# A small fill on GpSimd between two indirect transfers in a row, in a linear-attention and top-1 expert kernel

## The chip, the cores and the metric

The kernel runs on one core of a Trainium2 chip. The metric is the device time of one execution in microseconds, as the median of three runs. The engines are TensorE (PE in the profile), VectorE (DVE), ScalarE (ACT), GpSimd (POOL), and SyncE (SP), which here only starts transfers.

## What is computed

```python
# attention without a softmax, 8 batches x 8 heads, 576 rows of 64
kv  = np.einsum('bhsd,bhse->bhde', k, v)
out = np.einsum('bhsd,bhde->bhse', q, kv)
rms = np.sqrt(np.mean(out * out, axis=-1, keepdims=True) + 1e-06)
x   = (out / rms * g_norm)      # -> 4608 tokens of 512
# top-1 mixture of 8 experts, inner width 1024
logits = x @ w_gate
expert_idx = argmax(logits);  gate_w = softmax(logits) at that expert
for e in range(8):
    xe = x[expert_idx == e]
    out[expert_idx == e] = gate_w * (relu(xe @ w1[e]) @ w2[e])
```

So each token goes to one expert, and the tokens have to be sorted by expert on the way. The kernel does the sorting with indirect transfers, which GpSimd starts.

## The kernel before

**Attention stage.** The 4608 tokens are worked in 36 steps `s` of 128 tokens, nine for each pair of batches `P`. A step transposes queries, multiplies them with the batch's `kv` matrix (L339), squares and normalises (L359 to L378), and leaves a row of 512 half-precision numbers, token number and gate weight in a tile `xg`. Every three to five steps a `Route` object works out for its steps which expert each token takes and which rank it has there; `send` writes the row numbers to `sli`. Then `scatter(t)` (L450) sends one step's 128 rows to their places in `xs_scratch` in HBM, one indirect transfer for each of the 36 steps.

All engines are ordered by hand: each list of small functions (`mid`, `late`, `last`) is emitted step by step, and each engine works its own instructions in that order. Two other things are on GpSimd in this stage: `heads` (L256), four copies for each batch that reorder queries, and `pace` (L492), a one-column copy that waits until VectorE has reached the same step. For the first three pairs of batches every scatter has a `pace` ahead of it; for the last pair there is none.

**The seam.** The last two scatters belong to the route `tail` and follow the last step. The first gather may only start once every scatter has landed, since it reads `xs_scratch`. Meanwhile ScalarE and VectorE turn the weights of experts 0 and 1 to half precision, and TensorE runs 24 products on zeros (`zeros`, L127).

**Expert stage.** Eight jobs, one for each expert, and a ninth for what is left over. A job has up to five tiles of 128 tokens (640 rows). `rows(n)` starts the five gathers of job `n` (`gather`, L630) into five of 16 buffers `xe`; `rows(0)` and `rows(1)` are started at the seam, and job `n` starts `rows(n + 2)`. `flip` (L658, L661) transposes a gathered tile; `one` (L677, L684) is the first matrix product with the ReLU, 16 groups of four products for a job; `two` (L691, L696) is the second product, scales by the gate weight into `ys` (8 buffers) and scatters the rows to the output (L699). The five tiles of job `n + 1` are flipped inside the second half of job `n`'s first product, one after each group from the third on:

```python
for f in range(8):
    job.one(ws, f)
    ...
    if ws == job.halves - 1 and f >= 2 and flips:
        nxt.flip(flips.pop(0))
```

The weights come through SyncE, 2 MB each for `w1` and `w2` of an expert. Those of job 2 wait for the third flip of job 0 (`hold=True`). Job `n` starts those of job `n + 2`, and VectorE turns `w1` of job `n + 1` to half precision (L168). So GpSimd's list in the expert stage is: ten gathers, five output scatters of job 0, five gathers, five scatters of job 1, and so on, all indirect transfers and nothing else.

Of the kernel before, what the change touches and what calls it, by code (L numbers as in the profile page):

```python
# [12 lines left out]
F16 = mybir.dt.float16  # L13
# [15 lines left out]
def kernel(  # L29
# [11 lines left out]
    nc = tc.nc  # L41
# [49 lines left out]
    P_const = ctx.enter_context(tc.tile_pool(name="pconst", bufs=1))  # L91
# [28 lines left out]
    ]  # L120
    tabi = P_const.tile([128, 2, 32], I32, tag="tabi")
    zero16 = P_const.tile([128, 128], F16, tag="zero16")

    def zeros(t, n):

        for _ in range(n):
            nc.tensor.matmul(t, zero16, _bc(zero16, 1, 4), start=True, stop=True)  # L127
# [60 lines left out]
    with (  # L188
# [62 lines left out]
        def heads(b, j):  # L251

            if j == 0:
                qp[b] = PA.tile([128, 4, 8, 64], F32, tag="qp", bufs=2, name="qp")
            tv = ld["q", b].rearrange("p h (j d) -> p h j d", j=4)
            nc.gpsimd.tensor_copy(qp[b][:, j, :, :], tv[:, :, j, :])  # L256


# [126 lines left out]
        class Route:  # L385
# [61 lines left out]
                csum.append(cs)  # L447

            def scatter(self, t):
                nc.gpsimd.indirect_dma_start(  # L450
                    out=xs_views[9 * self.P + self.g0 + t],
                    out_offset=IndirectOffsetOnAxis(ap=self.sli[:, t:t + 1], axis=0),
                    in_=xgs[self.P][:, self.g0 + t, :].bitcast(I32),
                    in_offset=None,
                )
# [12 lines left out]
        for b in range(1, B):  # L468
            f = first_slot[b]
            n = 4 if b % 2 else 5  # L470
            plan = [[0, 1], [2, 3]] if n == 4 else [[0], [1, 2], [3]]
            o = 1 if b < 3 else 0
            for m, ii in enumerate(plan):
                for i in ii:
                    at(late, f - n + m + o, kv_mm, b, i)
            at(late, f - 3 + o, kv_copy, b)
            if o:
                at(mid, f - 1, kv_t, b)
                at(late, f - 1, kv_gate, b)
            else:  # L480
                at(late, f - 2, kv_t, b)
                at(mid, f - 1, kv_gate, b)
            for j in range(4):
                at(last, f - 4 + j // 2, heads, b, j)
            if b + 2 < B:
                at(last, f - 2, load_batch, b + 2)
# [33 lines left out]
        for j in range(4):  # L520
            heads(0, j)
# [39 lines left out]
        tail.ranks()  # L561
        tail.send()
        for t in range(2):
            tail.scatter(t)
        cp = PSA.tile([128, 8], F32, tag="misc", bufs=1, name="cp")
        nc.tensor.matmul(cp, ones, csum[-1], start=True, stop=True)
# [16 lines left out]
    with (  # L583
# [43 lines left out]
            nc.vector.tensor_copy(tabi[:, 1, 0:8], oi)  # L627

        def gather(xe, rows):
            nc.gpsimd.indirect_dma_start(  # L630
                out=xe.bitcast(I32),
                out_offset=None,
                in_=xs.ap(),
                in_offset=IndirectOffsetOnAxis(ap=rows, axis=0),
                bounds_check=E * N - 1,
                oob_is_err=False,
            )

        class Job:
# [48 lines left out]
            def two(self, t):  # L688
                yp = PSF.tile([128, D], F32, tag="yp", bufs=3, name="yp")
                for f in range(8):  # L690
                    nc.tensor.matmul(  # L691
                        yp, self.ht[:, f, t * 128:(t + 1) * 128], self.w.w2[:, f, :],
                        start=(f == 0), stop=(f == 7),
                    )
                ys = PF.tile([128, D], F32, tag="ys", bufs=8, name="ys")
                nc.vector.tensor_scalar(  # L696
                    ys, yp, self.xe[t][:, 514:516].bitcast(F32), None, op0=ALU.mult
                )
                nc.gpsimd.indirect_dma_start(  # L699
                    out=self.views[t],  # L700
                    out_offset=IndirectOffsetOnAxis(ap=self.idx[:, t:t + 1], axis=0),
                    in_=ys,
                    in_offset=None,
                    bounds_check=N - 1,
                    oob_is_err=False,
                )

        def left_over(t, t0, view):

            ev = nc.values_load(  # L710
                tabi[0:1, 0, bass.ds(t, 1)], engines=[ENG.SP],
                min_val=0, max_val=E - 1,
            )
            okm = PF.tile([128, 1], F32, tag="okm", bufs=2, name="okm")
            nc.vector.tensor_tensor(okm, pcol, nvf[:, bass.ds(t, 1)], op=ALU.is_lt)
            bgm = PF.tile([128, 1], F32, tag="bgm", bufs=2, name="bgm")
            nc.vector.tensor_scalar(bgm, okm, -BIG, BIG, op0=ALU.mult, op1=ALU.add)
            gi = PF.tile([128, 1], I32, tag="gi", bufs=2, name="gi")
            nc.vector.scalar_tensor_tensor(
                out=gi, in0=tabb[:, bass.ds(t, 1)], scalar=pcol, in1=bgm,  # L720
                op0=ALU.add, op1=ALU.add,
            )
            gather(xe_bufs[t0], gi)
            return Job([xe_bufs[t0]], Weights(bass.ds(ev, 1)), okm, bgm, [view])

        with tc.manual_schedule(engines=by_hand):
            jobs = []
            for n, e in enumerate(order):
                if e == "left":
                    jobs.append(None)  # L730
                    continue
                jobs.append(Job(
                    [xe_bufs[(n % 3) * CT + t] for t in range(CT)], W[n],
                    valid[:, e, :], bigm[:, e, :], out_views[e * CT:(e + 1) * CT],
                ))

            def rows(n):
                if n < len(order) and order[n] != "left":
                    for t in range(CT):
                        gather(jobs[n].xe[t], rowi[:, order[n], t:t + 1])  # L740

            rows(0)
            rows(1)
            zp = PSF.tile([128, 512], F32, tag="yp", bufs=3, name="yp")
            zeros(zp, 24)
            for t in range(3):
                jobs[0].flip(t)
                zeros(zp, 2)

            W[2].stage1(hold=True)  # L750
            W[2].stage2(hold=True)

            for n in range(len(order)):
                job = jobs[n]
                if n == 4:
                    jobs[E] = left_over(0, 3 * CT, out_views[E * CT])
                    W[E] = jobs[E].w
                nxt = jobs[n + 1] if n + 1 < len(order) else None
                rows(n + 2)
                flips = list(range(nxt.nt)) if nxt is not None else []  # L760
                for ws in range(job.halves):
                    for f in range(8):
                        job.one(ws, f)
                        if n == 0 and ws == 0 and f in (3, 6):
                            job.flip(3 + f // 6)
                        if ws == job.halves - 1 and f >= 2 and flips:
                            nxt.flip(flips.pop(0))
                        if n > 0 and ws == 0 and f % 2 == 1 and nxt is not None:
                            W[n + 1].half1(nc.vector, f // 2)
                            if f == 7 and n + 2 < len(order):  # L770
                                W[n + 2].stage1()
                for kk in range(max(job.nt, 4)):
                    if kk < job.nt:
                        job.two(kk)
                    if n > 0 and kk < 4 and nxt is not None:
                        W[n + 1].half2(kk)
                        if kk == 3 and n + 2 < len(order):
                            W[n + 2].stage2()
                    if n == 0 and kk == 1:
                        left_over_table()  # L780
# [42 lines left out]
```

## Time and profile before

| | |
|---|---|
| median of three runs | 306.58 us (305.64 to 307.6) |
| span of the profiled run | 303.6 us |
| mean granted TensorE clock | 0.975 |
| indirect transfers to `xs_scratch` (L450) | 36, mean 983 ns on GpSimd |
| gathers to `xe` (L630) | 40, mean 1012 ns, and one for the left-over job |
| indirect transfers to the output (L699) | 41, mean 1038 ns |
| fill of a 128x576 tile on GpSimd (L517) | 4, mean 573 ns |

The time of an indirect transfer on GpSimd is the time in which the engine is busy with it. The data arrive later; the profile gives that as "DMA to landing", counted from the start on the engine. A line of a timeline has the start and the duration in microseconds, the engine, the line of the kernel, the operation, its result and its operands, and in brackets how long the engine had been idle before it and what ended that. "<-issue" means that it waited for nothing that the profile shows. A line of the table by stretches has the stretch, its length, then for each engine the busy time and the number of instructions, the granted clock of TensorE (1.00 is full), and the busy share and rate of the DMA engines.

### The profile page before, as it was taken

To read this page: it belongs to the slowest core of one execution; us is meant where nothing else is said; L and a number is where in the kernel's file an instruction comes from. 1 tells how busy PE (TensorE), PEld (TensorE's weight loads), DVE (VectorE), ACT (ScalarE), POOL (GpSimd) and SP (SyncE) were. 2 spreads that over 40 slices of the span, in tenths; PEclk is the share of its full clock that TensorE was granted. 3 is DMA by queue.
4 is the path that set the end of the run, shared out by engine and by line. 5 is a ranking of instruction groups with operands and counts; after the bars stand their busy time and mean duration, and the time that the engine had idled before them with its cause. 6 is when DMAs were issued, how large, how long until landed. Compare 5 with 4: busy or idle time off the path is not lost.

```text
span 303.6 us, 6229 instructions
## 1 busy us (share of the span) xinstructions
PE 275.5 (91%) x2349; PEld 189.7 (62%) x2349; DVE 164.0 (54%) x431; ACT 159.2 (52%) x342; POOL 153.2 (50%) x205
## 2 busy tenths in 40 slices
PE   8697989899989987647979999999999999999993
PEld 3376877788878886513644756647566574665652
DVE  0024576768778777781237946445464553556140
ACT  1024556556564665488530674737657365672831
POOL 9332016438636764665762576457365663215052
PEclk9799999999999999869999999999999999999998
DMA  6999999999999999922894299979799898968421
GB/s 188 341 284 279 243 279 349 301 276 351 333 299 315 386 401 405 367 105 71 268 364 171 86 367 305 399 220 393 282 346 347 266 388 276 353 279 270 167 101 66
DMA packets 59790, 85.66 MB, mean 282 GB/s; under 512 B 16493, under 2 KB 41326, under 8 KB 59760
## 3 DMA queue, kind: packets, MB, share of 16 engines
q1 hardware_dynamic: 50512, 65.10, 67.7%
q0 software_dynamic: 6976, 18.96, 17.2%
q10 hardware_dynamic: 2272, 1.20, 1.5%
q8 instruction: 19, 0.31, 0.4%
q14 instruction: 11, 0.09, 0.1%
HBM read 71.71 MB, written 15.50 MB: 287 GB/s over the span
## 4 chain that ended last, share of the span: by engine, by line
PE 30%; issue 10%; DMA 9%; POOL 4%; POOLq 1%
PE yp L691 14%; PE hp L677 14%; DMA out_dram<-ys,idx 7%; POOL out_dram L699 2%; DMA xe<-xs_scratch,rowi 2%; PE xp L658 2%; POOL xe L630 2%; POOLq L818 0%; POOL xs_scratch L450 0%; POOLq L699 0%; POOLq L630 0%; POOLq L783 0%
## 5 line engine op out<-in xcount | busy, mean ns | idle before, releaser
L684 ACT ACTIVATE ht<-hp 128x320 f16<-128x320 f32 (+1 forms) x136 | 57.9, 428 | 70.0 <-PE hp L677 58.6
L677 PE MATMUL hp<-xt,w1e 128*128 128x320 f16 (+1 forms) x544 | 79.3, 294 | 0.1
L699 POOL DMA_INDIRECT out_dram<-ys,idx x41 | 42.6, 1038 | 65.7 <-DVE ys L696 56.6
L691 PE MATMUL yp<-w2e,ht 128*128 128x512 f16 x328 | 72.3, 379 | 0.0
L677 PEld LDWEIGHTS <-w1e 128*128 128x128 f16 x544 | 50.3, 98 | 18.8 <-issue 0.6
L696 DVE TENSOR_SCALAR ys<-yp,xe 128x512 f32<-128x512 f32 x41 | 30.6, 750 | 47.2 <-PE yp L691 47.2
L691 PEld LDWEIGHTS <-ht 128*128 128x128 f16 x328 | 32.1, 98 | 37.2
L339 PE MATMUL op<-kvs,qts 128*128 128x144 f32 (+1 forms) x320 | 45.5, 301 | 5.5 <-ACT kvt L292 2.5
L630 POOL DMA_INDIRECT xe<-xs_scratch,rowi x40 | 40.5, 1012 | 14.4 <-issue 10.2
L339 PEld LDWEIGHTS op<-kvs,qts 128*128 128x128 f32 (+1 forms) x320 | 38.1, 184 | 9.0 <-ACT kvt L292 3.1
L450 POOL DMA_INDIRECT xs_scratch<-xg,sli x36 | 35.4, 983 | 13.3 <-issue 10.8
L661 DVE COPY xt<-xp 128x512 f16<-128x512 f16 x41 | 17.4, 425 | 37.2 <-PE xp L658 37.2
L256 POOL COPY qp<-ld 128x512 f32<-128x512 f32 x32 | 18.5, 614 | 32.1 <-DMA ld<-in_q_dram 30.0
L179 ACT CAST w2e<-ws 128x1024 f16<-128x1024 f32 x32 | 31.0, 1042 | 0.0
L359 ACT ACTIVATE sq<-op 128x512 f32<-128x512 f32 x36 | 21.4, 593 | 14.2 <-PE op L339 13.9
L364 DVE TENSOR_REDUCE ms<-sq 128x8 f32<-128x512 f32 x36 | 24.4, 679 | 6.5 <-ACT sq L359 6.4
L326 ACT COPY qts<-qtp 128x512 f32<-128x512 f32 x36 | 20.9, 582 | 7.8 <-PE qtp L321 7.8
L275 PE MATMUL kvp<-ld 128*64 128x64 f32 x512 | 22.0, 228 | 3.4 <-DMA ld<-in_v_dram 3.3
L378 DVE TENSOR_TENSOR xg<-op,rinv 128x512 f16<-128x512 f32 x36 | 24.5, 681 | 0.3
L275 PEld LDWEIGHTS kvp<-ld 128*64 128x64 f32 x512 | 17.7, 137 | 8.5 <-issue 7.5
L368 ACT ACTIVATE lnt<-ms,epsb 128x8 f32<-128x8 f32 x36 | 10.9, 302 | 22.9 <-DVE ms L364 22.8
L168 DVE TENSOR_SCALAR w1e<-ws,g 128x1024 f16<-128x1024 f32 x32 | 22.2, 756 | 0.0
(92 smaller groups left out, 246.7 us busy)
## 6 DMA issues: line engine op xcount, KB each, us to landing
ws<-in_moe_w_dram SPq DMA_DIRECT2D x16, 2048.0 KB, 12.0
ld<-in_q_dram SPq DMA_DIRECT2D x8, 1024.0 KB, 11.1
ld<-in_k_dram SPq DMA_DIRECT2D x7, 1024.0 KB, 8.8
ld<-in_v_dram SPq DMA_DIRECT2D x7, 1024.0 KB, 10.9
ws<-in_moe_w_dram SPq DMA_DIRECT2D x4, 1024.0 KB, 16.8
kr<-in_k_dram SPq DMA_DIRECT2D x8, 128.0 KB, 9.2
ld<-in_k_dram SPq DMA_DIRECT2D x2, 512.0 KB, 7.5
ld<-in_v_dram ACTq DMA_DIRECT2D x2, 512.0 KB, 9.4
```

Of the source, the lines that this page charges most:

```text
L179: nc.scalar.copy(self.w2[:, 2 * kk:2 * kk + 2, :], self.s2[:, 2 * kk:2 * kk + 2, :])
L275: nc.tensor.matmul(kvp[64 * hh:64 * hh + 64, i, :], lhs, rhs, start=(j == 0), stop=(j == 4),)
L339: nc.tensor.matmul(op[c, i // 2, c0:c0 + 144], qts[s][:, i, c], kvs[:, i, :], start=True, stop=True,)
L364: nc.vector.reduce_sum(ms, sq, axis=AXX)
L378: nc.vector.tensor_tensor(xg[:, r, 0:512].rearrange("p (c i h n) -> p c i h n", c=2, i=2, h=2), ox, _bc(r4, 4, 64), op=ALU.mult,)
L450: nc.gpsimd.indirect_dma_start(out=xs_views[9 * self.P + self.g0 + t], out_offset=IndirectOffsetOnAxis(ap=self.sli[:, t:t + 1], axis=0), i ...
L630: nc.gpsimd.indirect_dma_start(out=xe.bitcast(I32), out_offset=None, in_=xs.ap(), in_offset=IndirectOffsetOnAxis(ap=rows, axis=0), bounds_ ...
L677: nc.tensor.matmul(hp, self.w.w1[:, kk, f * 128:(f + 1) * 128], self.xt[:, kk, ws * wd:(ws + 1) * wd], start=(kk == 0), stop=(kk == 3),)
L684: nc.scalar.activation(self.ht[:, f, ws * wd:(ws + 1) * wd], hp, ACTF.Relu)
L691: nc.tensor.matmul(yp, self.ht[:, f, t * 128:(t + 1) * 128], self.w.w2[:, f, :], start=(f == 0), stop=(f == 7),)
L696: nc.vector.tensor_scalar(ys, yp, self.xe[t][:, 514:516].bitcast(F32), None, op0=ALU.mult)
L699: nc.gpsimd.indirect_dma_start(out=self.views[t], out_offset=IndirectOffsetOnAxis(ap=self.idx[:, t:t + 1], axis=0), in_=ys, in_offset=None ...
```

## The change

A tile `breath` of 128x576 half-precision numbers is added, which nothing reads. `spaced()` is called ahead of each indirect transfer. If another indirect transfer was the last thing of this kind on GpSimd, it fills `breath` with zeros first. The list `near` remembers that; it is cleared ahead of each `heads` copy, ahead of each of the two scatters of `tail`, and ahead of each of the five first gathers, so that these have no fill. A `pace` copy does not clear it. The purpose is to hold two indirect transfers on GpSimd apart, except where the next stage is waiting for them.

```diff
+    breath = P_const.tile([128, 576], F16, tag="breath")
+    near = []
+
+    def spaced():
+
+        if near:
+            nc.gpsimd.memset(breath, 0.0)
+        near[:] = [1]
...
             tv = ld["q", b].rearrange("p h (j d) -> p h j d", j=4)
+            near.clear()
             nc.gpsimd.tensor_copy(qp[b][:, j, :, :], tv[:, :, j, :])
...
             def scatter(self, t):
+                spaced()
                 nc.gpsimd.indirect_dma_start(
                     out=xs_views[9 * self.P + self.g0 + t],
...
         for t in range(2):
+            near.clear()
             tail.scatter(t)
...
         def gather(xe, rows):
+            spaced()
             nc.gpsimd.indirect_dma_start(
                 out=xe.bitcast(I32),
...
+                spaced()
                 nc.gpsimd.indirect_dma_start(
                     out=self.views[t],
...
                     for t in range(CT):
+                        if n == 0:
+                            near.clear()
                         gather(jobs[n].xe[t], rowi[:, order[n], t:t + 1])
```

## The prediction

> **What bounds the kernel now.** I read the page first: PE is busy for 91% of the span and POOL for 50%, so the question is not whether GpSimd has room on average but in which stretch something waits for it. So next the table by stretches.
>
> ```profile
> 129.00:136.60 7.60, 3.72 (x12) 1.51 (x13) 6.80 (x29) 6.18 (x9) 5.08 (x5) 0.64 0.29 106
> 136.60:144.00 7.40, 6.08 (x30) 2.30 (x27) 0.81 (x4) 6.63 (x11) 4.04 (x4) 0.91 0.23 73
> 152.00:158.00 6.00, 4.32 (x39) 2.67 (x40) 2.38 (x9) 2.18 (x5) 4.78 (x5) 1.00 1.02 359
> 158.00:166.80 8.80, 8.80 (x43) 4.02 (x41) 5.76 (x18) 0.44 (x1) 2.27 (x3) 1.00 0.57 208
> 185.20:195.00 9.80, 9.80 (x85) 7.36 (x84) 6.00 (x14) 6.55 (x15) 6.90 (x7) 1.00 1.02 379
> 250.00:268.80 18.80, 18.80 (x129) 11.57 (x127) 9.52 (x20) 11.02 (x21) 5.24 (x5) 1.00 0.92 329
> ```
>
> From 158 us on TensorE (first busy column) has no gap and runs at full clock: a job takes 18.44 us (second products start at 176.77, 195.22, 213.66 in the chain of waits). What happens at the seam, from about 122 to 158 us, moves the whole rest of the kernel one for one. GpSimd's timeline there:
>
> ```profile
> 122.03 0.18 POOL L492 COPY tick<-lr 128x1 f32<-128x1 f32 x1 [0.60 <-DVE lr L372]
> 122.70 0.98 POOL L450 DMA_INDIRECT xs_scratch<-xg,sli  x1 [0.49 <-issue]
> 123.98 0.96 POOL L450 DMA_INDIRECT xs_scratch<-xg,sli  x1 [0.30 <-issue]
> ...
> 129.94 0.96 POOL L450 DMA_INDIRECT xs_scratch<-xg,sli  x1 [1.21 <-DVE cs L446]
> ...
> 135.17 1.07 POOL L450 DMA_INDIRECT xs_scratch<-xg,sli  x1 [0.30 <-issue]
> 138.80 1.04 POOL L630 DMA_INDIRECT xe<-xs_scratch,rowi  x1 [2.56 <-issue]
> ```
>
> Ten scatters run one behind the other, every 1.27 us (0.96 and a gap of 0.30), with one wait in between. The next line, the first gather, comes 2.56 us after the end of the last, for that is when the last has landed. Now TensorE:
>
> ```profile
> 133.46 7.57 PE L127 MATMUL yp<-zero 128*128 128x512 f16 x24 [0.26 <-DVE cnt L567]
> 141.59 0.40 PE L658 MATMUL xp<-ch,xe 128*128 128x128 f16 x4 [0.56 <-DMA xe<-xs_scratch,rowi]
> 154.24 0.40 PE L658 MATMUL xp<-ch,xe 128*128 128x128 f16 x4 [0.35 <-DMA xe<-xs_scratch,rowi]
> 155.96 0.40 PE L658 MATMUL xp<-ch,xe 128*128 128x128 f16 x4 [0.78 <-DMA xe<-xs_scratch,rowi]
> 157.39 0.40 PE L658 MATMUL xp<-ch,xe 128*128 128x128 f16 x4 [0.49 <-DMA xe<-xs_scratch,rowi]
> ```
>
> It waits for the first gather at 141.59, and for the last three gathers of job 1 at 154 to 157. Those five gathers start at 145.36 to 150.57, every 1.30 us; the flips that wait tell their landing, 6.2 to 6.8 us later (150.57 to 157.34 for the last). Even the first of them, with next to no gather ahead of it, needs as long; this is its landing, against that of the gather at 142.76, before the weights of job 2 start at 145.4:
>
> ```profile
> DMA to landing us min/median/max: 6.7/6.7/6.7
> DMA to landing us min/median/max: 2.9/2.9/2.9
> ```
>
> So the wait in the queues beside a weight load is a delay, not a backlog of gathers, and a later start is a later landing.
>
> **What the Trainium skill says.** "DMA: Bandwidth & Descriptors", section on the anatomy of one DMA on the GpSimd path: some 2 us are fixed, mostly the confirmation of the last byte. The trace agrees in kind, 2.5 to 2.9 us to landing when the queues are quiet; beside weights it is 6.2 (median of the gathers). "SBUF — State Buffer", section "Who interferes with whom": a VectorE operation in a two-port mode and a GpSimd operation shut each other out of a shared port pair. The copies to half precision (L168, single source, SBUF to SBUF, 747 ns for 1024 elements) fit that, and the output scatters that fall beside them take 1.24 us instead of 0.98. "TensorE: Matmul & The Clock Gate", Part 1: an idle window of some 3.4 us halves the clock, and a busy one restores it. Here the clock was 0.50 from 131.6 to 138 after four nearly empty microseconds.
>
> **The change part by part.** The order of GpSimd's instructions shows where fills fall: between all scatters of the last two full groups (eight fills from 122.03 on, none ahead of the two of `tail`), ahead of gathers 6 to 10 and 11 to 15, and ahead of every later indirect transfer. Nothing is removed. A fill waits for nothing but the fill before it, long done; the indirect transfers behind it in the queue are what it holds up.
>
> *Price of a fill.* The fill of 128x576 in full precision (L517) is 0.574 us, that of 128x516 in half precision (L519) 0.517 us, so 0.9 to 1.0 ns an element in either; I take 0.574. It also takes the place of part of the 0.30 us gap: where a `tick` of 0.19 us stands between two transfers (75.19 to 75.54), it starts at once and the gap after it is 0.15, so it costs its own time less 0.15. A fill costs 0.574 - 0.15 = 0.42 us; bounds 0.27 (all of the gap used) and 0.57 (none).
>
> *Attention up to 120 us: nothing.* A fill comes after a `tick` that mostly waits for VectorE (19.4 us of waiting in all), and slots with `heads` copies have none. A slot with fill needs 0.19 + 0.57 + 0.15 + 0.98 = 1.9 us of the 2.5 us or so that a step takes.
>
> *Seam: +2.3 us.* The first of the ten starts 0.91 instead of 0.67 us after its tick (+0.24). Seven further fills add 7 x 0.42 = 2.94. The wait at 129.94 is swallowed: that interval was 2.16 instead of 1.27, so -0.89. Sum 2.29. Behind them stand the two of `tail`, which have no fill but stand in the same queue, then the landing, then the first gather. All go 2.3 later. ScalarE's weight copies end at 143.2 either way and would not have been waited for. Bounds: 0.12 + 7 x 0.27 - 0.89 = 1.1, and 0.39 + 7 x 0.57 - 0.89 = 3.5.
>
> *Gathers of job 1: +1.7 us.* The fifth of them has five fills ahead of it since the first gather, 5 x 0.42 = 2.1 us. The weights still load beside it (to 155.1 and 162.5 before). Its latency was 6.77 against 6.2 for the third, so I give 0.4 back for fewer gathers in the queue. Bounds 0.8 and 2.8. These flips set when job 0's second product can start.
>
> *Later jobs: nothing.* In 18.44 us GpSimd has five gathers and five scatters, 10 x 1.30 and about 0.4 for the long ones, 13.4 us; ten fills make it 17.6. Where job 4 has a gather more it is 19.3, made good in the jobs without gathers. Some 0.5 us a job may come from fills shut out beside L168. Gathers are used 10 us or more after they start, and `ys` has eight buffers. Among scatters that wait for `ys` (idle 0.74 each time) the fill stands in that idle time.
>
> *Tail: +0.2 us.* The last five scatters of job 7 run behind each other after a wait (292.53 to 296.41), so fills shift the last of them by 1.3 to 1.7 us, to 298; but the very last, of the left-over job, waits for VectorE (299.91), and its fill ends at about 299.3. Bounds 0 and 1.
>
> *Clock.* TensorE's idle time ahead of the first flip grows from 0.6 to 2.9 us. If the clock halves, the first hidden products lose some 1.7 us, which they win back while they wait for job 1's gathers. No cost taken.
>
> Sum: 2.3 + 1.7 + 0.2 = 4.2; 306.58 + 4.2 = 310.8 us.
>
> **Rivals.**
> (a) *The gathers of job 1 are limited by throughput, not by delay.* They land 1.4 to 1.7 us apart, about as fast as fills would let them start. Then their fills cost nothing, and 2.3 + 0.2 gives 309.1, near the bound of what can be told. For it: the growing latency 6.2, 6.6, 6.8. Against: 6.7 for the first.
> (b) *The clock drops in the sparse stretch.* Job 1's flips then come every 1.7 us with about 0.95 us of work each. If that counts as idle, the second product runs at half clock for about 3.4 us: another 1.7, 312.5. Against it: at 0.72 busy (152 to 158) the clock stayed at 1.00.
> (c) *Hidden or faster.* If transfers apart from each other land sooner, or the fill runs in the gap, the kernel takes 305 to 307. What speaks for it is only that the gap of 0.30 is longer than the 0.15 after a tick, and that gathers land late at 6.2 us. But they are late beside weights, whose bytes stay the same, and TensorE has no gap after 158 us that could be won; to end faster by over 1% the seam itself would have to become 3 us shorter.
> (d) *GpSimd becomes the bound of the jobs.* If fills are shut out for a whole 0.75 us at a time, a job costs GpSimd over 18.44 us; with 1 us too much in each of six jobs still only the last scatters are late, since gathers are ahead: 312 to 314.
>
> **How the numbers follow.** The forecast 0.47, (a) 0.2, (b) 0.12, (d) 0.05, (c) 0.16, of which 0.05 ends faster by over 1%. Over 1% slower begins at 309.65: the forecast nearly whole, half of (a), all of (b) and (d), some 0.75. Faster 0.05, within 1% 0.2. Range 307.6 to 313.2: below it most of (c) is left out, above it the upper bounds of the fill's price.
>
> **What would show it.** Right: fills of 0.57 us, a scatter every 1.7 us from 122 to 135, the first gather near 141.1, the flips of job 1 that wait near 156 to 161, a second product of job 0 that starts near 162.2 instead of 158.2, and jobs of 18.44 us after it. Wrong: a first gather before 140, landings under 5 us, gaps of TensorE in later jobs, or a last scatter that starts over 1 us after its `ys`.

## The result, and the profile after

| | before | after |
|---|---|---|
| time, median | 306.11 us (305.36 to 307.6) | 317.8 us (316.63 to 318.23) |
| ratio | | 1.037, interval 1.0319 to 1.042 |
| span of the profiled run | 303.6 us | 314.8 us |
| TensorE clock, mean | 0.975 | 0.943 |

The direction was right and the size was not: 11.3 us more (0.037 x 306.11) instead of 4.2. Ratios here and below compare undisturbed runs alone, while the medians are those of all runs. GpSimd's timeline shows where the fills stand at the seam (columns as in the prediction):

```profile
129.24 0.99 POOL L461 DMA_INDIRECT xs_scratch<-xg,sli  x1 [0.16 <-issue]
130.22 0.60 POOL L130 MEMSET breath<- 128x576 f16 x1
130.99 0.97 POOL L461 DMA_INDIRECT xs_scratch<-xg,sli  x1 [0.17 <-issue]
...
140.57 1.01 POOL L130 MEMSET breath<- 128x576 f16 x1
141.74 1.22 POOL L461 DMA_INDIRECT xs_scratch<-xg,sli  x1 [0.17 <-issue]
...
144.58 0.96 POOL L461 DMA_INDIRECT xs_scratch<-xg,sli  x1 [0.30 <-issue]
148.11 1.03 POOL L643 DMA_INDIRECT xe<-xs_scratch,rowi  x1 [2.57 <-issue]
```

The first line is the 27th scatter, the first of the ten in a row. Before, it started at 122.70. So 6.5 us are lost ahead of the stretch in which the prediction looked for the loss. From here to the first gather it is 18.87 us, before 16.10. TensorE at the seam:

```profile
151.07 0.61 PE L671 MATMUL xp<-ch,xe 128*128 128x128 f16 x4 [4.88 <-DMA xe<-xs_scratch,rowi]
...
164.91 0.40 PE L671 MATMUL xp<-ch,xe 128*128 128x128 f16 x4 [0.90 <-DMA xe<-xs_scratch,rowi]
...
167.50 0.40 PE L671 MATMUL xp<-ch,xe 128*128 128x128 f16 x4 [0.57 <-DMA xe<-xs_scratch,rowi]
168.27 1.89 PE L704 MATMUL yp<-w2e,ht 128*128 128x512 f16 x8
```

It waits 4.88 us for the first gather (0.56 before), and two flips of job 1 wait instead of three. The second product of job 0 starts at 168.27 instead of 158.17. After job 1 the jobs are 18.44 us apart as before, and the table by stretches has TensorE full in them:

```profile
158.00:168.30 10.30, 8.59 (x74) 5.55 (x72) 3.71 (x14) 5.08 (x12) 9.33 (x12) 1.00 1.03 403
260.00:278.80 18.80, 18.80 (x131) 11.61 (x130) 10.74 (x21) 10.97 (x21) 17.14 (x22) 1.00 0.92 320
```

GpSimd's column (the fifth busy one) is 17.14 of 18.80 us: nearly full, and no bound yet. So the 11.2 us between the spans are made of: up to the 27th scatter 6.54, from there to the first gather 2.77, to job 0's second product 0.79, to job 1's 0.23, and from job 7's second product (286.38, now 296.71) to the last scatter (299.91, now 311.15) 0.91. The sum is 11.24. This is one trace against one other; further down the stretches are compared over several.

### The profile page after: what moved, and what is told of

Same layout as the page of the kernel before. It is cut to its first block, busy times and chain, and to the rows that moved or that the text cites. A ratio compares the mean times of both kernels' runs of the same rounds, so it can differ in the third digit from the quotient of the medians.

```text
span 314.8 us, 6330 instructions
## 1 busy us (share of the span) xinstructions
PE 282.7 (90%) x2349; PEld 196.7 (62%) x2349; DVE 173.3 (55%) x431; ACT 159.0 (50%) x342; POOL 214.8 (68%) x305
## 4 chain that ended last, share of the span: by engine, by line
PE 31%; DMA 10%; POOL 6%; DVE 4%; issue 3%; POOLq 1%
PE yp L704 15%; PE hp L690 14%; DMA out_dram<-ys,idx 8%; POOL xe L643 2%; PE xp L671 2%; DMA xe<-xs_scratch,rowi 2%; POOL breath L130 2%; DVE w1e L177 1%; POOL xs_scratch L461 1%; POOL out_dram L713 1%; DVE ys L709 1%; POOLq L834 0%; DVE xt L674 0%; DVE cm L626 0%; DVE cm L619 0%
## 5 line engine op out<-in xcount | busy, mean ns | idle before, releaser
L130 POOL MEMSET breath<- 128x576 f16 x100 | 62.0, 620 | 0.0
L713 POOL DMA_INDIRECT out_dram<-ys,idx x41 | 44.1, 1076 | 23.9 <-DVE ys L709 16.8
L349 PE MATMUL op<-kvs,qts 128*128 128x144 f32 (+1 forms) x320 | 48.4, 313 | 6.5 <-DVE xg L388 3.3
L349 PEld LDWEIGHTS op<-kvs,qts 128*128 128x128 f32 (+1 forms) x320 | 40.6, 193 | 10.3 <-ACT sq L369 4.7
L177 DVE TENSOR_SCALAR w1e<-ws,g 128x1024 f16<-128x1024 f32 x32 | 30.9, 1025 | 0.0
L285 PE MATMUL kvp<-ld 128*64 128x64 f32 x512 | 23.2, 237 | 4.9 <-DMA ld<-in_v_dram 4.9
L285 PEld LDWEIGHTS kvp<-ld 128*64 128x64 f32 x512 | 18.7, 145 | 9.9 <-issue 9.0
## 6 DMA issues: line engine op xcount, KB each, us to landing
ws<-in_moe_w_dram SPq DMA_DIRECT2D x16, 2048.0 KB, 11.4
ld<-in_v_dram SPq DMA_DIRECT2D x7, 1024.0 KB, 11.2
```

The source lines that it names most:

```text
L130: nc.gpsimd.memset(breath, 0.0)
L177: eng.tensor_scalar(self.w1[:, kk, :], st, g2, 1.0, op0=ALU.mult, op1=ALU.mult,)
L285: nc.tensor.matmul(kvp[64 * hh:64 * hh + 64, i, :], lhs, rhs, start=(j == 0), stop=(j == 4),)
L349: nc.tensor.matmul(op[c, i // 2, c0:c0 + 144], qts[s][:, i, c], kvs[:, i, :], start=True, stop=True,)
L713: nc.gpsimd.indirect_dma_start(out=self.views[t], out_offset=IndirectOffsetOnAxis(ap=self.idx[:, t:t + 1], axis=0), in_=ys, in_offset=None ...
```

## The experiments

The theory after the result: the tile itself costs in the attention stage, by where it puts the tiles behind it. It has 1152 bytes a partition and lies in SBUF ahead of `ws` and `ld`, into which weights, queries, keys and values are loaded, and of others. The rival: the fills hold up the attention stage.

The runs fell on five chips. On the one of the first group and of the last run the kernel before takes 306 us; below it is called the ordinary chip. On the other four it takes 332 to 337 us, which is the subject of the third part. The expectations name theories by letters: Q, L and F are explained in the first group, A and P in the second with after_1536. "27th", "gather" and "product" stand for the start of the 27th scatter, of the first gather and of job 0's second product in the profiled run, in us.

### Parts of the change (before 305.64 us)

| run | us | ratio (interval) | 27th | gather | product | last scatter |
|---|---|---|---|---|---|---|
| before (first profile) | | | 122.70 | 138.80 | 158.17 | 299.91 |
| again | 316.38 | 1.0346 (1.027 to 1.0421) | 128.28 | 147.22 | 168.00 | 311.18 |
| tile_only | 310.68 | 1.0156 (1.0084 to 1.0228) | 128.65 | 144.45 | 162.87 | 304.61 |
| scatter_fills | 312.91 | 1.0239 (1.0176 to 1.0301) | 126.86 | 145.91 | 165.39 | 307.14 |
| expert_fills | 312.20 | 1.0205 (1.0142 to 1.0268) | 127.42 | 143.09 | 164.01 | 307.03 |

The changed kernel a second time, with no edit.

> The changed kernel once more, for a second trace. Q (queue): the fills cost what stands behind them on GpSimd, 2.96 us at the seam, 0.8 and 0.2 at the gathers, 0.9 at the tail, 4.9 in all; the other 6.4 us of the first trace arose before the first fill (at 55.2 us), where TensorE ran at half clock from 26 to 46 us. Then this trace shows 4.9 us again from the seam on, and the attention part can come out otherwise. L (layout): the early 6.4 us belong to the kernel and come again in the same place: clock 0.50 from about 26 to 46 us, total 317 to 318.

The tile alone, filled once at the start:

```diff
     def spaced():
-        if near:
-            nc.gpsimd.memset(breath, 0.0)
-        near[:] = [1]
+        pass
...
+        nc.gpsimd.memset(breath, 0.0)
```

> The tile breath is allocated and filled once at the start (0.57 us among the other fills there); no fill stands between transfers. Q: 306.1 +- 1. L: the place of all later tiles, shifted by 1152 bytes a partition, is the cause of the early loss: about 312. If the whole change were layout: 318.

The fills ahead of scatters to `xs_scratch` alone (23), by taking `spaced()` out of `gather` and `two`:

> Fills only between the scatters of the attention stage (23), none at gathers and output scatters. Q: the seam alone, +2.3 to 3.0, 309. L: 309 and the early loss, 315. A third theory, F (fills disturb the attention stage itself, by way of steps that wait for GpSimd): the attention stage ends later than 122 us at the tick ahead of the last ten scatters, with TensorE or VectorE waiting for GpSimd.

The fills ahead of gathers and output scatters alone (77), by taking it out of `scatter`:

> Fills only ahead of gathers and output scatters (77), none among the scatters of the attention stage. Q: +0.8 + 0.2 + 0.9 = 1.9 us, 308. L: 308 and the early loss, 314. F: nothing early, 308.

The tile without a fill between transfers costs 5.0 us (310.68 - 305.64; by the interval 2.6 to 7.0), nearly half of the whole loss. It arises ahead of the 27th scatter, which starts 5.95 us later than in the trace of before. Up to the second product 1.25 us are won back, and from there to the last scatter it is 141.74 us, to the hundredth what it was before. Against this trace the changed kernel's last scatter is 6.54 us later: 0.59 arise up to the 27th scatter, 3.07 from there to the first gather, 1.74 to job 0's second product, 0.23 in job 1 and 0.91 at the end.

All four runs came out some 1 to 2 us below what L expected and 4 to 5 above Q. By the medians the parts don't add up: 5.0 us for the tile, 2.2 for the fills ahead of scatters and 1.5 for the others make 8.7 of the 10.7 that again lost. The ratio of each run has an interval of some 2 us to either side, so the shares are not known better than that.

With the fifteen fills ahead of it the 27th scatter starts at 129.24, 128.28 and 126.86 (after, again, scatter_fills), without them at 128.65 and 127.42 (tile_only, expert_fills): no difference within the spread. So the fills don't hold up the attention stage. The table by stretches shows what goes with the loss. Before:

```profile
20.00:30.00 10.00, 7.96 (x91) 7.01 (x91) 4.03 (x9) 4.83 (x11) 1.33 (x3) 1.00 1.14 272
30.00:40.00 10.00, 8.86 (x109) 7.92 (x109) 5.93 (x17) 5.20 (x15) 0.93 (x2) 1.00 1.12 262
```

tile_only:

```profile
20.00:30.00 10.00, 6.33 (x81) 5.43 (x81) 3.61 (x7) 3.85 (x11) 1.50 (x3) 1.00 1.17 247
30.00:40.00 10.00, 9.21 (x91) 8.40 (x86) 5.19 (x15) 3.99 (x10) 0.76 (x2) 0.83 1.20 240
```

The last two columns are the busy share of the DMA engines and the rate. The engines are no less busy than before and move 8 to 9% less (247 against 272, 240 against 262 GB/s). The stage lives on the loads of `q`, `k` and `v`: TensorE does 81 and 91 products instead of 91 and 109, and its clock falls to 0.83. Here it waits for a load in tile_only, and here in the changed kernel:

```profile
24.13 0.69 PE L283 MATMUL kvp<-ld 128*64 128x64 f32 x16 [1.71 <-DMA ld<-in_v_dram]
25.47 0.69 PE L285 MATMUL kvp<-ld 128*64 128x64 f32 x16 [2.87 <-DMA ld<-in_v_dram]
```

In all, these products wait 3.3 us for `ld` in before, 6.9 in tile_only and 4.9 in the changed kernel, where the clock then stays at 0.50 from 30 to 40 us.

### The place of the tiles

To tell the place from the tile, the kernel before gets nothing but an unused pad, filled once at the start (64, 128 or 768 half-precision columns, so 128, 256 or 1536 bytes), and the changed kernel a pad of 192 columns, which makes its shift 1536 bytes.

```diff
+    pad = P_const.tile([128, 64], F16, tag="pad")
...
+        nc.gpsimd.memset(pad, 0.0)
```

| run | before there | us | ratio (interval) |
|---|---|---|---|
| shift_128 | 336.33 | 340.91 | 1.0212 (1.0088 to 1.0337) |
| shift_256 | 336.33 | 335.84 | 0.9996 (0.9954 to 1.0038) |
| shift_1536 | 336.33 | 336.37 | 1.0030 (0.9987 to 1.0074) |
| after_1536 | 336.33 | 314.34 | 0.9394 (0.9260 to 0.9529) |
| shift_128_again | 336.83 | 340.14 | 1.0153 (1.0114 to 1.0192) |

> The kernel before with an unused tile of 128 bytes, which gives the later tiles the same place within 512 bytes as the 1152 bytes of breath do. A: 310 to 311. P: 310 to 311 as well. If the size of the shift counts and not its rest: 306.

> The kernel before with an unused tile of 256 bytes. A with 256 as the length that counts: 306. A with 512: something else than before, 306 to 311. P: 310 to 311.

> The kernel before with an unused tile of 1536 bytes a partition behind zero16, filled once at the start; no fill between transfers. A: 306, as before. P: 310 to 311, as the tile alone with 1152 bytes.

> The changed kernel with all its fills, and a second unused tile of 384 bytes a partition behind breath, so that the tiles behind both lie 1536 bytes (3 x 512) further than before instead of 1152; the place within 512 bytes is that of the kernel before again. A (alignment: the place within 512 bytes of the tiles that loads write decides their rate in the attention stage): rate from 10 to 40 us back at 260 to 315 GB/s, attention stage as before (tick ahead of the last ten scatters near 122 us), and only the fills' cost is left: 306 + 5.5 = 311.5. P (the plain presence of one more tile, or where it lies, not the place within 512 bytes): 316 to 318 as the changed kernel.

> The kernel before with a pad of 128 bytes a partition ahead of the later tiles and no fill. Theory (placement): 4.5 to 5 us more than before on any chip, ratio 1.013 to 1.018, rate of the loads lower from 10 to 40 us (about 302, 250, 240 GB/s instead of 313, 273, 260), 27th scatter 4 us or more later. Rival (an effect of the one chip): ratio 1.00 to 1.005.

The times in us that were expected here hold for the ordinary chip, so only the ratios can be read. A shift by 128 bytes, with no other edit, costs 2.1 and 1.5%, some 7 and 5 us; both intervals exclude 1, and the second ratio is the expected one. Shifts by 256 and 1536 bytes, multiples of 256, cost nothing that shows. So P is out, and of A the form with 256 is left; 1152 is 4.5 times 256. The size of the tile isn't what counts, since 1536 is more than 1152. In the trace of shift_256 the loads move 315, 287 and 269 GB/s from 10 to 40 us, in that of shift_128 on the same chip 302, 263 and 237. Over all runs of this document, those of the next part too, the mean rate from 10 to 40 us is 263 to 273 GB/s in the seven traces with a shift of 128 or 1152 bytes, and 276 to 290 in the thirteen with none or a multiple of 256.

All tiles behind the new one move together, so which of them has to lie where is not shown, nor what other shifts than these would do. Why multiples of 256 bytes matter is not shown either. The Trainium skill, "DMA: Bandwidth & Descriptors", section "How a descriptor splits into AXI transactions", says that a piece which doesn't start on a multiple of 256 bytes is read from the multiple below it, and that the bytes in between are fetched unused and still cost a part of the transfer. That agrees with the unit, though the page speaks of reading and here the place moves where the loads write. And in the compiled program `ld` lies 160 bytes past such a multiple before and 32 past one after, off it in both; by the page's count of unused bytes the place after should be the cheaper one, and the runs show the opposite. `ws` moves from 128 bytes past a multiple onto one, and its loads of 2 MB are no slower: they land after 11.4 us at the median, before after 12.0.

### Which fills cost, and a surprise

after_1536 was 22 us faster than before by the medians on its chip, which nothing in the first profile had announced. The next runs take the aligned kernel (shift 1536) and keep a part of the fills, by a count of the calls:

```diff
-        if near:
+        if near and (kind != "xs" or n <= 26):
```

That is aligned_no_seam; aligned_seam keeps `kind == "xs" and n > 26`, aligned_late `kind == "in" and n > 10 or kind == "out" and n <= 35`.

| run | fills | before there | us | ratio (interval) | 27th | gather | product |
|---|---|---|---|---|---|---|---|
| aligned_again | 100 | 332.88 | 314.31 | 0.9439 (0.9372 to 0.9507) | 125.75 | 144.65 | 165.36 |
| aligned_seam | 8 | 332.88 | 334.03 | 1.0007 (0.9975 to 1.0039) | 124.56 | 143.54 | 172.49 |
| aligned_no_seam | 92 | 332.88 | 312.14 | 0.9414 (0.9342 to 0.9487) | 123.72 | 139.46 | 160.49 |
| aligned_late | 66 | 332.88 | 317.68 | 0.9531 (0.9456 to 0.9606) | 126.42 | 142.08 | 168.33 |
| short_fill, 16 columns | 100 | 336.83 | 336.62 | 0.9986 (0.9955 to 1.0018) | 125.42 | 141.27 | 171.92 |
| aligned_third | 100 | 336.83 | 313.61 | 0.9296 (0.9247 to 0.9344) | 124.71 | 143.75 | 164.96 |
| aligned_fourth | 100 | 332.23 | 313.43 | 0.9425 (0.9351 to 0.9498) | 124.86 | 143.93 | 164.56 |
| half_fill, 288 columns | 100 | 332.23 | 309.98 | 0.9353 (0.9294 to 0.9412) | 124.98 | 142.04 | 162.17 |
| half_no_seam, 288 columns | 92 | 306.12 | 307.25 | 1.0030 (1.0004 to 1.0057) | 122.63 | 139.03 | 158.71 |

> The changed kernel with a pad of 384 bytes behind the new tile, so that all later tiles lie 1536 bytes further on instead of 1152, run a second time. Theory (placement): on a chip where the kernel before takes 306 us, only the price of the fills is left, seam +2.9, gathers of job 1 +0.8, later +0.2, tail +0.9: 4.8 us more than before, ratio 1.015 to 1.018, first gather 3 us later than before. Where the kernel before itself is slow in the expert stage (336 us in the last set of runs): 311 to 315 us, ratio 0.93 to 0.94. Rival (the fills themselves delay the attention stage): the ratio on an ordinary chip stays at 1.035 and the 27th scatter starts over 3 us later than before.

> As aligned_again, with fills only ahead of the eight scatters of the last pair of batches that follow each other at the seam (27th to 34th). Theory: the first gather starts 2.3 to 3 us later than before and everything after it as much later; +2.5 to +3 us on an ordinary chip, ratio about 1.009. Rival (the seam's fills are hidden in the landing of the last scatter): first gather within 1 us of before, ratio 1.00. Where the kernel before is slow in the expert stage, this one is as slow (no fill there): ratio 1.00 to 1.01.

> As aligned_again, without the fills ahead of those eight scatters; all other fills kept. Theory: first gather within 0.5 us of before, second product of job 0 about 0.8 to 1.7 us later, tail another 0.9: +1.7 to +2.8 us on an ordinary chip, ratio 1.006 to 1.009; the sum of this excess and that of aligned_seam is that of aligned_again. Rival (fills cost wherever they stand, by their number): 68 of 76 spread fills, so close to aligned_again, ratio 1.014 or more. Where the kernel before is slow in the expert stage, 309 to 312 us.

> As aligned_again, with fills only where nothing waits for what stands behind them: ahead of gathers from job 2 on and of output scatters up to job 6 (66 fills). Theory: within 0.7 us of before on an ordinary chip, ratio 0.998 to 1.003, jobs of 18.44 us. Rival (GpSimd becomes the bound of the jobs, or fills slow VectorE's copies so that weights come late): over 1 us more. Where the kernel before is slow in the expert stage: 308 to 312 us, faster than both kernels, with the exception of job 1's gathers, which follow each other without a fill and may hold up the first job by up to 4 us.

**The price of the seam's fills** comes from the 27th scatter to the first gather: 18.90 and 18.98 us with them (aligned_again, aligned_seam), 15.74 and 15.66 without (aligned_no_seam, aligned_late). So they cost some 3.2 us on a chip of the other sort, and they are not hidden in the landing. The first group says the same: 18.87, 18.94 and 19.05 with them (after, again, scatter_fills), 15.80 and 15.67 without (tile_only, expert_fills). Only against before, where this stretch took 16.10, is it 2.77: there a scatter waited 1.21 us for VectorE, of which more could be swallowed than of the 0.75 in tile_only.

**The surprise.** aligned_seam is as slow as before there, aligned_no_seam and aligned_late are not: what makes the kernel fast on such a chip are the fills in the expert stage, for aligned_late has no others. There is no trace of before itself from such a chip. VectorE in shift_256, a kernel without fills, and behind it TensorE and ScalarE:

```profile
158.63 0.42 DVE L663 COPY xt<-xp 128x512 f16<-128x512 f16 x1 [10.33 <-PE xp L660]
...
163.01 0.42 DVE L663 COPY xt<-xp 128x512 f16<-128x512 f16 x1 [3.83 <-remote]
...
162.66 4.32 PE L679 MATMUL hp<-xt,w1e 128*128 128x320 f16 x16 [4.91 <-issue]
162.17 0.44 ACT L686 ACTIVATE ht<-hp 128x320 f16<-128x320 f32 x1 [5.94 <-remote]
```

VectorE's copy of the fourth flip of job 0, which in before on the ordinary chip starts at 147.82, comes at 158.63, since TensorE's flip is late; "remote" is a releaser that the trace can't name. TensorE stands for 4.91 us and ScalarE for 5.94, while GpSimd runs 15 gathers in a row from 141.5 to 160.8. In the stretch from 145 to 161 us this is before, on the ordinary chip:

```profile
145.00:161.00 16.00, 14.15 (x107) 8.66 (x107) 4.87 (x19) 6.97 (x16) 10.03 (x11) 1.00 0.95 329
```

and this is shift_256:

```profile
145.00:161.00 16.00, 8.75 (x50) 4.82 (x49) 2.13 (x10) 2.42 (x6) 12.13 (x13) 0.75 0.81 283
```

TensorE does half of its work (50 against 107 products), though the DMA engines have room (share 0.81). Its jobs are then mostly 20 to 24 us apart instead of 18.44. aligned_late, whose gathers of job 1 have no fills, shows the edge of it: its first gather to its second product takes 26.25 us, with fills there (aligned_no_seam) 21.03. That made it 317.68 us, more than the 312 and up to 4 that were expected; the other three came out as expected for such a chip, to 0.2 us.

Is it time that is missing between two transfers, or just another instruction? The next two kernels write less of the tile, and its size is a multiple of 256 bytes, to keep the places:

```diff
-    breath = P_const.tile([128, 576], F16, tag="breath")
+    breath = P_const.tile([128, 128], F16, tag="breath")
...
-            nc.gpsimd.memset(breath, 0.0)
+            nc.gpsimd.memset(breath[:, 0:16], 0.0)
```

For half_fill the numbers are 640 and 288.

> The changed kernel with a tile of 256 bytes a partition, of which each fill writes 16 columns instead of 576, so that no later tile comes to lie off a multiple of 256 bytes and a fill takes about 0.1 us. Where the kernel before takes 306 us: theory (cost by the length of the fill): the seam's eight fills fit into the gap of 0.30 us, so within 1 us of before, ratio 0.998 to 1.004. Rival (each instruction between two transfers costs a fixed time): seam at least +1.5 us, ratio over 1.005. Where the kernel before takes over 330 us: if another instruction between two transfers is what counts, 306 to 311 us; if the time between them counts (transfers 1.7 instead of 1.3 us apart), 322 us or more.

> The same kernel as aligned_again (long fills, later tiles 1536 bytes further on). Where the kernel before takes 306 us: theory (placement is 5 us of the loss, fills the rest): 310 to 311.5 us, ratio 1.013 to 1.018; rival (fills delay the attention stage by themselves): 314 us or more, ratio over 1.028. Where the kernel before takes over 330 us: 311 to 315 us.

> The same kernel as aligned_again and aligned_third (long fills, later tiles 1536 bytes further on). Where the kernel before takes 306 us: theory (placement is 5 us of the loss, fills the rest) 310 to 312 us, ratio 1.013 to 1.02; rival (fills delay the attention stage by themselves) 314 us or more, ratio over 1.028. Where the kernel before takes over 330 us: 311 to 315 us, as twice before.

> The changed kernel with a tile of 1280 bytes a partition, of which a fill writes 288 columns instead of 576 (about 0.3 us; transfers about 1.43 us apart instead of 1.72). Where the kernel before takes 306 us: seam 8 x (0.3 - 0.15) - 0.89 + 0.2, so 0.5 us, and 307 us or so, ratio 1.000 to 1.008. Where the kernel before takes over 330 us: if some room between two transfers is enough, 308 to 313 us, faster than both; if the room must be as long as 0.7 us, 322 us or more.

The short fill fits into the gap: its transfers stay 1.30 us apart, and it is as slow as before, on a chip where the long fill takes 313.61. The half fill sets them 1.51 us apart, and TensorE does 102 products in the same stretch:

```profile
145.00:161.00 16.00, 12.80 (x102) 8.18 (x103) 3.94 (x17) 5.71 (x14) 13.93 (x21) 1.00 0.83 288
```

So one more instruction isn't enough, a longer one is, and 0.5 us between the end of one transfer on GpSimd and the start of the next was enough on the chip where it ran. That it is the time and not the writing is likely but not shown: no run had a pause of that length without a write. What is held up in these chips while transfers follow at 0.3 us stays open, and so does why before on the ordinary chip has no such stands.

**The last run** takes half fills and none at the seam, and it fell on the ordinary chip.

> As half_fill, without the fills ahead of the eight scatters at the seam. Where the kernel before takes 306 us: gathers of job 1 +0.4, tail +0.5, so 306.5 to 307.5 us, ratio 1.000 to 1.004. Where the kernel before takes over 330 us: half_fill less 8 x 0.2, so 308 to 309 us, the fastest of all (ratio 0.925 to 0.933); rival (the seam's fills also keep the attention stage from standing still): 311 us or more.

307.25 against 306.12: within the expectation, 0.3% slower. Of the two terms expected, the gathers of job 1 cost 0.31 us in the trace (0.4 expected), the tail nothing (0.5 expected). Its tile of 1280 bytes is five times 256. It still has 15 half fills in the attention stage, and its 27th scatter starts at 122.63, that of before at 122.70. On the same chip tile_only had it at 128.65. So placement costs 6 us in that trace, and half fills in that stage nothing. No version beat the kernel before on the ordinary chip. On the others half_fill is the fastest that ran; half_no_seam did not run there. The full fill with aligned tiles was not timed on the ordinary chip.

## Why the prediction was wrong, point by point

**Attention up to 120 us: nothing. This is the step that failed.** It priced the fills, rightly at nothing, and didn't price the tile. The line `breath = P_const.tile(...)` moved all tiles behind it by 1152 bytes. That costs 5.0 us (tile_only), about 45% of the whole loss of 11.3; in the profiled run the 27th scatter was 6.5 us late. Neither the main sum nor any rival held a word on it. The fills alone were priced too low as well, but less: against the trace of tile_only they cost 6.54 us instead of 4.2, mostly at the seam and in the tail.

**Price of a fill: 0.42 us.** About right. Most fills take 0.57 to 0.60 us, the gap after them is 0.16 to 0.17, and scatters come every 1.73 us instead of 1.27, so 0.46. The mean over all is longer, since some are shut out:

```profile
L130 POOL MEMSET breath<- 128x576 f16 x100 | 62.0, 620 | 0.0
```

**Seam: +2.3 us.** 0.24 of it was to come before the 27th scatter starts; for the rest, 2.05, it was 2.77 against before, and 3.2 where less waiting could be swallowed. What the 2.77 has more: six intervals of 0.04 too little are 0.2, and the rest is the fill at 140.57 of 1.01 us and the scatter of 1.22 behind it (0.4 and 0.25 too long); a landing 0.1 shorter gives a little back. Fill and scatter lie beside four copies of `w1` to half precision on VectorE, from 139.97 to 143.45. The prediction named such a shut-out only for later jobs, by the Trainium skill's "SBUF — State Buffer", section "Who interferes with whom". The trace agrees with that section in both directions, for the copies became longer too, 747 ns at the median before:

```profile
L177 DVE TENSOR_SCALAR w1e<-ws,g x32: 732/1092/1435, 140.0 to 291.4; 128x1024 f16<-128x1024 f32 x32
```

The columns in the middle are minimum, median and maximum in ns. The longer copies cost nothing that shows: from job 1's second product on the jobs stay 18.44 us apart.

**Gathers of job 1: +1.7 us.** About right, though the first pair of traces hides it with 0.79. From the first gather to the second product it is 20.16, 20.78 and 20.92 us with these fills (after, again, expert_fills), and 19.37, 18.42 and 19.48 without (before, tile_only, scatter_fills): 1.5 more by the means. The fifth gather starts 2.27 us later after the first one (14.04 against 11.77), where 2.1 was predicted. Its flip comes 5.35, 5.94 and 6.11 us after its start with the fills and 6.82, 5.85 and 6.94 without, so some 0.7 is given back instead of 0.4. Most of a later start is a later landing, and rival (a), by which these fills cost nothing, didn't come true.

**Later jobs: nothing.** 0.23 in job 1, then 18.44 us each. Rival (d) didn't come true.

**Tail: +0.2 us.** It was 0.91. The fill is done before `ys` is, as predicted, and yet the last scatter starts 1.19 us after `ys`, before 0.28. The prediction had named a start over 1 us after `ys` as a sign that it is wrong:

```profile
309.06 0.61 POOL L130 MEMSET breath<- 128x576 f16 x1
311.15 0.98 POOL L713 DMA_INDIRECT out_dram<-ys,idx  x1 [1.48 <-DVEq L799]
```

The fill ends at 309.67 and `ys` at 309.96. again and expert_fills show the same 0.9 us. In half_no_seam, whose last fill ends 1.2 us ahead of `ys`, the scatter follows after 0.28 us as before. So a fill that ends just ahead of the release goes with a late start; why isn't shown.

**Clock.** It halved around the first flips, as allowed for: 0.50 from 150 to 155 us, where before has 1.00. What that costs by itself isn't told apart; expert_fills kept 1.00 there and still took 20.92 us to its second product. Rival (b)'s drop among job 1's flips did not come: the clock is 1.00 from 158 us on.

**Rival (c), hidden or faster.** Not on the chip that was predicted for. On the others kernels with fills in the expert stage were 5 to 7% faster than before. That is not what (c) argued, and the first profile can't show it.

## What to carry to other kernels

A new tile is a change of all addresses behind it: before its instructions are priced, ask where it moves the tiles that bulk loads land in, and try a second pad; here shifts by multiples of 256 bytes cost nothing, and 128 and 1152 bytes did. An instruction between transfers costs its time less the gap that it fills (here 0.6 us less 0.15), and only where somebody waits at the end of that queue. On four of five chips here the kernel with rows of indirect transfers 0.3 us apart took 332 to 337 us instead of 306, so time such a kernel on more than one. And compare a stretch over several traces before a step is called wrong: one pair put job 1's gathers at 0.79 us, six traces at 1.5.

## What was not expected of the hardware

- A shift of the tiles by 128 or 1152 bytes goes with slower loads, 263 to 273 GB/s from 10 to 40 us against 276 to 290 with none or a multiple of 256, and costs 1.5 to 2.1% (5 to 7 us).
- The same kernel without fills takes 306 us on one chip and 332 to 337 on four others. There, in a kernel without fills, VectorE got nothing to do for 10 us and TensorE did half of its work while indirect transfers started every 1.30 us. With half fills they start every 1.51 us, the stands are gone, and the time is 310 us.
- Beside full fills on GpSimd VectorE's copies to half precision take 1092 ns at the median instead of 747, and a fill is itself stretched from 0.60 to 1.01 us.
